# An attention and GLU block on one core: the attention output normalized in its feature layout, the softmax sums spread by DMA, and the GLU weights loaded in 15 parts

## The chip, the core and the metric

The kernel runs on one core of a Trainium2 chip. The core has five engines that each work through a list of instructions in order: TensorE (PE; its weight loads are listed as PEld), VectorE (DVE), ScalarE (ACT), GpSimd (POOL) and SyncE (SP), which in this kernel only issues DMAs. They wait for each other by semaphores. PSUM, the memory that TensorE writes, has eight banks of 128 x 512 fp32. The metric is the device time of one execution in microseconds; the profile shows one execution, and its span is the time from its first to its last instruction.

## What is computed

One sequence of 2048 tokens, 640 features, 32 heads of 20 features, GLU width 1728, all in bf16:

```python
def _A_ref(x, wqkv, wo):                 # 32 heads, Dh = 20
    q, k, v = (x @ wqkv) split by head
    scores = einsum("bhqd,bhkd->bhqk", q, k) * (Dh ** -0.5)
    p = softmax(scores, axis=-1)
    o = einsum("bhqk,bhkd->bhqd", p, v)
    return o.reshape(B, S, D) @ wo
def _B_ref(x, w_gate, w_up, w_down):
    h = gelu(x @ w_gate) * (x @ w_up)
    return h @ w_down
h  = x + _A_ref(layernorm(x), A_wqkv, A_wo)
h2 = h + _B_ref(layernorm(h), B_w_gate, B_w_up, B_w_down)
```

## The kernel before

The kernel is written as a list of operations with their readers and writers, assumed durations and priorities. A planner in Python (`Sched.schedule`) plays them through when the program is built and fixes the order of every engine's list; `Sched.emit` then writes the lists with the semaphore waits that the data need. No time is fixed on the chip: what the planner assumes decides only in which order things stand. An assumed time that is longer makes the planner put more other work ahead of the instruction that waits. For a DMA there are two such times: `dur`, the time of the issue on SP, and `lat`, the time from the issue to the landing. Where PE would be little used, the planner adds filler matmuls ("warm", which stand in the profile as matmuls of `kt_all` with itself, and "pad").

The queries are cut into seven chunks of 512, 512, 256, 256, 256, 128 and 128 tokens. A chunk is worked through in slots: eight groups of four heads for a chunk of 512, two groups together for 256, four for 128, in all 32 slots. In a slot a score tile is 128 keys by 512 query columns; four heads sit in four row quarters of PE (L911). Tiles are taken in units of three and two tiles, 693 units in the kernel. ACT computes the exponential of a unit (a line of a helper, L357, `pts` or `rege` from `ps` with 1536 or 1024 columns). Some tiles are exponentiated by DVE instead (L832 and the TENSOR_SCALAR lines of L357). PE then multiplies by V (L357, 21 columns: 20 features and a column of ones, so that row 20 of each quarter holds the sum of the exponentials). The result for four heads, `O`, collects in PSUM bank 6 as 4 x 32 rows by 512 columns.

When a slot is complete, `epilogue` runs: DVE copies bank 6 to `osb` (fp32, two buffers), PE transposes it in four fp32 transposes (L976), DVE takes the reciprocal of the sums (L982) and multiplies (L985) into `o_nat`, tokens in the partitions.

When all slots of a chunk are complete, `post` runs for it as background of the next chunk: `o_nat` is transposed back to `oT` (features in the partitions), by PE for chunk 0 and for the last, by a transposing DMA otherwise; then the `wo` matmuls (L632) and the residual (L1021), LayerNorm, a transposing DMA of the result to `hnT`, the gate matmuls (L1053, copied out by DVE at L1088), one group of gelus on ACT, the up matmuls (L1053, multiplied at L1099), the down matmuls (L1110), the second residual (L1114) and the store. ACT has to load another table for gelu and again for the exponential. For the last chunk (the tail) the transposes are PE's and the gelu reads PSUM (L1075).

The projections of K, Q and V for groups beyond the first are background of chunk 0: their rows go through DRAM (`k_rows`, `q_rows`) and come back in the layout of the score matmuls, and a bound per query (`bounds`, L724) is added as one more row. All these DMAs are issued by SP in order. In slot 7 the GLU weights are loaded over the place of the QKV weights by three large DMAs and a small one for the last 64 rows of `w_down`, which shares its key and semaphore with the third.

Of the kernel before, what the change touches and what calls it, by code (L numbers as in the profile page):

```python
# [301 lines left out]
D = 640  # L302
# [33 lines left out]
def bass_sequential_preLN__mha_block__glu_gated_geglu__prompt_kernel(  # L336
# [12 lines left out]
    with ExitStack() as es:  # L349
# [3 lines left out]
        def sb(name, shape, dt=BF16):  # L353
            return es.enter_context(nc.sbuf_tensor(name, shape, dt))
# [5 lines left out]
        def c_mm(n, passes=1):  # L360
            return 0.004 + passes * n / 2400.0
# [28 lines left out]
        pts = sb("pts", [128, PR * 512])  # L390
        osb = sb("osb", [128, 2, 512], FP32)
        rc = sb("rc", [128, 2, 16], FP32)
        o_nat = sb("o_nat", [128, 4, D])
        sq = sb("sq", [128, 512])
        xn_t = sb("xn_t", [128, 2, D])

# [51 lines left out]

        kdr = nc.dram_tensor("k_rows", [D, S], BF16, kind="Internal").ap()
        qdr = nc.dram_tensor("q_rows", [4, D, 512], BF16, kind="Internal").ap()  # L450
        odr = nc.dram_tensor("bounds", [4, H, 512], BF16, kind="Internal").ap()

        PS = es.enter_context(nc.psum_tensor("ps", [128, 8 * 512], FP32))
# [135 lines left out]
        def dma_transposes(src, rkeys, dst, wkey, after=()):  # L589
            op("sp", I("dma_start_transpose", dst, src), 1.25, P_EPI, reads=rkeys, writes=[wkey], sem=f"xp{wkey[1]}", lat=2.0, after=after)  # L590
# [364 lines left out]
        def base(c):  # L955
            n = CHUNKS[c][1]
            if n == 128:
                return 2 + (c == len(CHUNKS) - 1)
            return 2 * (c % 2) if n < 512 else 0

        def epilogue(s_, bk):
            s = s_ % 2
            c, gs = slots[s_]
            nq = CHUNKS[c][1]
            nt = nq // 128
            op("dve", I("tensor_copy", osb[:, s, :], PS[:, 512 * 6:512 * 7]), c_dve(512), P_QK,
               reads=[("O", s_)], writes=[("osb", s)], rel=[bk])
            b2 = Bank(*BG[c])
            key = ("bk", sc_id())
            aft = set()  # L970
            tb = base(c)
            for g in gs:
                for tt in range(nt):
                    aft.update(sc.rd.get(("on", g, tb + tt), ()))
            for tt in range(4):
                op("pe", lambda eng, tt=tt: eng.transpose(bank(b2)[:, tt * 128:(tt + 1) * 128],  # L976
                                                          osb[:, s, tt * 128:(tt + 1) * 128], identf[:]),
                   c_mm(128, 2.5), P_EPI, mode="full", reads=[("osb", s), "identf"], writes=[key], acq=[b2] if tt == 0 else [],
                   after=tuple(aft) if tt == 0 else ())
            bv = lambda: bank(b2).rearrange("p (t j e) -> p t j e", t=4, j=4)  # L980
            rcv = rc[:, s, :].rearrange("p (t j) -> p t j", t=4)
            op("dve", lambda eng: eng.reciprocal(rcv, bv()[:, :, :, DH]), 0.17, min(P_EPI, sc.ev), reads=[key], writes=[("rc", s)])  # L982
            for gi, g in enumerate(gs):
                dst = o_nat[:, tb:tb + nt, g * 80:(g + 1) * 80].rearrange("p t (j e) -> p t j e", j=4)
                op("dve", lambda eng, gi=gi, dst=dst: eng.tensor_tensor(  # L985
                    dst, bv()[:, gi * nt:(gi + 1) * nt, :, 0:DH],
                    rcv[:, gi * nt:(gi + 1) * nt, :].unsqueeze(3).to_broadcast([128, nt, 4, DH]), ALU.mult),
                   c_dve(80 * nt), min(P_EPI, sc.ev), reads=[key, ("rc", s)], writes=[("on", g, tb + tt) for tt in range(nt)],
                   rel=[b2] if gi == len(gs) - 1 else [])
# [10 lines left out]
        def post(c, banks, tail):  # L1000
# [3 lines left out]
            tb = base(c)  # L1004
            hb = 1792 * tb
            first = tuple(e_ops) + tuple(last_qk[0]) + tuple(d_ops) if c == 0 else ()
            for tt in range(tb, tb + nt):
                t = q0 // 128 + tt - tb
                i = t % 2
                if tail or c == 0:  # L1010
                    transposes(o_nat[:, tt, :], [("on", g, tt) for g in range(NG)], oT[:, :, tt * 128:(tt + 1) * 128],
                               ("hnT", tt), banks, P_EPI, "act" if tail else "dve", after=first)
                else:
                    dma_transposes(o_nat[:, tt, :], [("on", g, tt) for g in range(NG)], oT[:, :, tt * 128:(tt + 1) * 128],
                                   ("hnT", tt), after=first)
                for hf in range(2):
                    bk = Bank(*banks)
                    key = ("bk", sc_id())
                    list(chain(bk, key, 320, [(oT[:, a, tt * 128:(tt + 1) * 128], wo[:, a, hf * 320:(hf + 1) * 320])
                                              for a in range(NA)], [("hnT", tt), "wo"], p, after=(sc.lw[("h", tt, hf)],)))  # L1020
                    op("dve", lambda eng, bk=bk, tt=tt, hf=hf, i=i: eng.tensor_tensor(  # L1021
                        h_sb[:, tt, hf * 320:(hf + 1) * 320], bank(bk, 320), h_sb[:, tt, hf * 320:(hf + 1) * 320], ALU.add),
                       c_dve(320), p, reads=[key, ("h", tt, hf)], writes=[("h", tt, hf)], rel=[bk], after=first)
                ln_stats(h_sb[:, tt, :], t, [("h", tt, 0), ("h", tt, 1)], p)
# [22 lines left out]
            def mms(k, w, wkey, after):  # L1047
                bk, key = Bank(*banks), ("bk", sc_id())
                for fi in range(min(fn_, NF - k * fn_)):
                    f = k * fn_ + fi  # L1050
                    for a in range(NA):
                        st = fi == 0 and a == 0
                        op("pe", lambda eng, a=a, f=f, fi=fi: eng.matmul(  # L1053
                            bank(bk)[:, fi * nq:(fi + 1) * nq], w[:, a, F0[f]:F0[f] + 128], hnT[:, a, 128 * tb:128 * tb + nq],
                            start=(a == 0), stop=(a == NA - 1)),
                           c_mm(nq), p, mode="full", util=nq / 2400.0, reads=hk + [wkey], writes=[key], acq=[bk] if st else [],
                           after=after if st else ())
                return bk, key

# [6 lines left out]
            def hkeys(k):  # L1066
                return [("ha", u) for u in range((hb + 512 * k) // 256, (hb + 512 * k + cols(k)) // 256)]
# [34 lines left out]
            for tt in range(tb, tb + nt):  # L1102
                t = q0 // 128 + tt - tb
                i = t % 2
                for hf in range(2):
                    bk = Bank(*banks)
                    key = ("bk", sc_id())
                    for f in range(NF):
                        o = hb + f * nq + (tt - tb) * 128
                        op("pe", lambda eng, f=f, o=o, hf=hf, bk=bk: eng.matmul(  # L1110
                            bank(bk, 320), ha_f[:, o:o + 128], wd[:, f, hf * 320:(hf + 1) * 320],
                            start=(f == 0), stop=(f == NF - 1)), c_mm(320), p, mode="full", util=0.133, reads=hkeys(f // fn_) + ["wd", "wdz"],
                           writes=[key], acq=[bk] if f == 0 else [], after=hdone[-2:] if f == 0 else ())
                    op("dve", lambda eng, bk=bk, tt=tt, hf=hf, i=i: eng.tensor_tensor(  # L1114
                        ob[:, i, hf * 320:(hf + 1) * 320], bank(bk, 320), h_sb[:, tt, hf * 320:(hf + 1) * 320], ALU.add),
                       c_dve(320), p, reads=[key, ("h", tt, hf)], writes=[("ob", i, hf)], rel=[bk], after=first)
                op("sp", I("dma_start", out_hbm[t * 128:(t + 1) * 128, :], ob[:, i, :]), 0.08, p,
                   reads=[("ob", i, 0), ("ob", i, 1)], sem=f"out{i}", lat=2.5)
# [17 lines left out]
        for s_, (c, gs) in enumerate(slots):  # L1136
            if c == 0:
# [16 lines left out]
                    q_bound(cc, tuple(range(NA)), 0, NG, BG0, P_BG)  # L1154
                if g == 7:
                    wr = tuple(w_readers)
                    load(wg, B_w_gate.rearrange("(a p) f -> p a f", p=128), "wg", 11.0, after=wr)
                    load(wu, B_w_up.rearrange("(a p) f -> p a f", p=128), "wu", 16.0, after=wr)
                    load(wd[:, 0:NF - 1, :], B_w_down[0:(NF - 1) * 128, :].rearrange("(a p) d -> p a d", p=128),
                         "wd", 21.0, after=wr)  # L1160
                    r0 = (NF - 1) * 128 - F0[-1]
                    load(wd[r0:128, NF - 1, :], B_w_down[(NF - 1) * 128:DFF, :], "wd", 2.6, after=wr)
                    op(POOL, I("memset", wd[0:r0, NF - 1, :], 0.0), 0.8, P_BG, writes=["wdz", "pool"], after=wr)
            while ui < len(units) and uslot[ui] <= s_:
                unit(ui)
# [37 lines left out]
```

## Time and profile before

| | |
|---|---|
| time, median of 3 runs (lowest to highest) | 912.77 us (912.53 to 921.97) |
| the profiled execution: time, span | 915.09 us, 913.2 us |
| mean granted TensorE clock | 0.993 |
| busy in the span: PE, PEld, DVE, ACT, POOL | 861.3, 371.0, 651.7, 859.8, 33.2 us |
| instructions | 24238 |
| exponentials on ACT, first start to last end | 36.1 to 873.2 us |
| bytes moved by DMA | 34.43 MB, mean 38 GB/s |
| fp32 transposes of the epilogue | 128, 26.8 us of PE busy time |
| issue to landing: row stores of 128 KB, load of 640 KB (median) | 1.7 to 1.9 us, 5.2 us |

Busy times of PE overlap with each other, since matmuls are pipelined: a PE that is busy for a whole stretch may still have room. The granted clock is the share of full speed that the throttle let TensorE have. A wait is put down to what ended it. Line numbers are those of the kernel before; L357 is the helper through which many operations are recorded, so that these are told apart by their tiles.

### The profile page before, as it was taken

How to read it: one execution, taken by the hardware profiler on the slowest of the kernel's cores; microseconds unless marked ns; L12 is line 12 of the kernel's file. 1: busy time of each engine (PE TensorE's matmuls, PEld its weight loads, DVE VectorE, ACT ScalarE, POOL GpSimd, SP SyncE). 2: the span in 40 equal slices, each digit the busy share in tenths (PEclk: the TensorE clock that was granted, in tenths of full speed). 3: DMA queues.
4: the chain of work that ended last, by engine and by line, in shares of the span. 5: the costliest groups of instructions: out<-in, count | busy, mean ns of one | idle time of the engine just before them, and what ended most of it. 6: DMA issues, size and time to landing. Idle time of an engine off the chain costs nothing.

```text
span 913.2 us, 24238 instructions
## 1 busy us (share of the span) xinstructions
PE 861.3 (94%) x10905; PEld 371.0 (41%) x10905; DVE 651.7 (71%) x1210; ACT 859.8 (94%) x775; POOL 33.2 (4%) x117
## 2 busy tenths in 40 slices
PE   3999999999999999999999998999999999999998
PEld 2532222222232222222344443333444456666677
DVE  7838797888888968877777785665556766654453
ACT  6699999989999989999999999999999999999960
POOL 5000000000001000000000010000001100010100
PEclk9999999999999989999999999999999999999999
DMA  7211020230100380000100101000101001000100
GB/s 259 86 46 32 13 56 6 61 89 22 50 8 12 64 295 1 1 1 1 31 9 17 38 2 31 1 1 2 38 23 45 17 2 24 25 17 10 39 9 23
DMA packets 39519, 34.43 MB, mean 38 GB/s; under 512 B 19436, under 2 KB 36936, under 8 KB 39416
## 3 DMA queue, kind: packets, MB, share of 16 engines
q1 hardware_dynamic: 39416, 32.89, 12.8%
q8 instruction: 85, 1.39, 0.6%
q14 instruction: 18, 0.15, 0.1%
HBM read 20.12 MB, written 8.09 MB: 31 GB/s over the span
## 4 chain that ended last, share of the span: by engine, by line
PE 46%; ACT 45%; DVE 5%; DMA 2%; issue 0%; SPq 0%; DVEq 0%
ACT pts L357 34%; PE ps L911 13%; PE ps L357 11%; ACT rege L357 10%; PE ps L1053 7%; PE ps L632 7%; PE ps L1110 6%; DMA regw<-in_A_wqkv_dram 1%; DVE rege L832 1%; DVE rege L357 1%; DMA rege<-in_A_x_dram 1%; DVE qt_all L832 1%; ACT L357 1%; PE ps L976 1%; DVE qt_all L357 1%; PE ps L577 0%
## 5 line engine op out<-in xcount | busy, mean ns | idle before, releaser
L357 ACT ACTIVATE pts<-ps 128x1536 bf16<-128x1536 f32 x578 | 652.0, 1252 | 14.8 <-PE ps L911 8.8
L911 PE MATMUL ps<-qt_all,kt_all 32*128 32x256 bf16 (+2 forms) x3584 | 322.4, 290 | 20.2 <-ACT pts L357 11.2
L911 PEld LDWEIGHTS ps<-qt_all,kt_all 32*128 32x128 bf16 x3584 | 102.9, 92 | 236.9 <-ACT pts L357 130.2
L832 DVE TENSOR_SCALAR rege<-ps 128x512 int16<-128x512 f32 x200 | 137.4, 688 | 73.3 <-PE ps L911 71.2
L357 ACT ACTIVATE rege<-ps 128x1536 bf16<-128x1536 f32 x115 | 173.2, 1506 | 1.6 <-PE ps L911 1.1
L1053 PE MATMUL ps<-rege,regw 128*128 128x256 bf16 (+2 forms) x980 | 154.5, 290 | 3.8 <-DVE rege L1099 2.3
L357 PE MATMUL ps<-pts,v_all 128*21 128x256 bf16 (+2 forms) x2472 | 135.0, 288 | 0.0
L357 PE MATMUL ps<-rege,v_all 128*21 128x512 bf16 (+2 forms) x1564 | 127.9, 316 | 1.4 <-DVE rege L357 1.0
L832 DVE TENSOR_SCALAR qt_all<-ps 128x512 int16<-128x512 f32 x116 | 79.8, 688 | 49.1 <-PE ps L911 48.4
L1053 PEld LDWEIGHTS ps<-rege,regw 128*128 128x128 bf16 x980 | 74.3, 98 | 57.8 <-issue 26.1
L357 DVE TENSOR_SCALAR rege<-rege 128x2048 int16<-128x2048 int16 x132 | 88.8, 685 | 2.4 <-PE ps L357 1.1
L632 PE MATMUL ps<-regw 128*128 128x512 bf16 (+1 forms) x360 | 87.5, 352 | 2.0 <-DVE rege L832 0.9
L1110 PE MATMUL ps<-regw,rege 128*128 128x320 bf16 x448 | 80.1, 301 | 1.1 <-DVE rege L832 0.5
L357 PEld LDWEIGHTS ps<-pts,v_all 128*21 128x21 bf16 x2472 | 54.3, 91 | 34.6 <-issue 28.3
L357 PEld LDWEIGHTS ps<-rege,v_all 128*21 128x21 bf16 x1564 | 41.3, 91 | 44.0 <-issue 24.4
L357 PE MATMUL ps<-qt_all,v_all 128*21 128x256 bf16 (+2 forms) x1048 | 53.7, 284 | 2.1 <-DVE qt_all L357 2.0
L1099 DVE TENSOR_TENSOR rege<-rege,ps 128x512 bf16<-128x512 bf16 (+1 forms) x53 | 36.0, 680 | 27.2 <-PE ps L1053 27.2
L1110 PEld LDWEIGHTS ps<-regw,rege 128*128 128x128 bf16 x448 | 37.1, 98 | 29.9 <-issue 13.8
L632 PEld LDWEIGHTS ps<-regw 128*128 128x128 bf16 x360 | 29.2, 99 | 47.6 <-issue 26.3
L1088 DVE CAST rege<-ps 128x512 bf16<-128x512 f32 (+1 forms) x53 | 36.1, 680 | 16.2 <-PE ps L1053 16.0
L357 DVE TENSOR_SCALAR qt_all<-rege 128x2048 int16<-128x2048 int16 x70 | 47.0, 686 | 0.7
L357 DVE TENSOR_SCALAR qt_all<-qt_all 128x2048 int16<-128x2048 int16 x69 | 46.3, 685 | 1.7 <-PE ps L357 1.3
(92 smaller groups left out, 483.7 us busy)
## 6 DMA issues: line engine op xcount, KB each, us to landing
rege<-in_A_x_dram SPq DMA_DIRECT2D x6, 640.0 KB, 5.2
q_rows<-regw SPq DMA_DIRECT2D x20, 128.0 KB, 1.7
out_dram<-rege SPq DMA_DIRECT2D x16, 160.0 KB, 1.9
regw<-in_B_w_gate_dram SPq DMA_DIRECT2D x1, 2160.0 KB, 10.6
regw<-in_B_w_up_dram SPq DMA_DIRECT2D x1, 2160.0 KB, 15.6
regw<-in_B_w_down_dram SPq DMA_DIRECT2D x1, 2080.0 KB, 21.6
kt_all<-k_rows SPq DMA_DIRECT2D x12, 160.0 KB
qt_all<-q_rows SPq DMA_DIRECT2D x12, 160.0 KB
```

The source lines that it names most:

```text
L357: return lambda eng: getattr(eng, method)(*args, **kwargs)
L632: yield op("pe", lambda eng, l=l, r=r, k=k: eng.matmul(bank(bk, n), l, r, start=(k == 0), stop=(k == len(steps) - 1)), c_mm(n), prio, mode ...
L832: d_ops.append(op("dve", lambda eng: eng.tensor_scalar(v[:, 512 * h:512 * h + 512], bank(b), EXP_MUL, -32000.0, ALU.mult, ALU.max), c_dve( ...
L911: return lambda eng: eng.matmul(out()[:, kk * nq:(kk + 1) * nq], kt_all[32 * j:32 * j + 32, g, kt * 128:(kt + 1) * 128], qt_all[32 * j:32 ...
L976: op("pe", lambda eng, tt=tt: eng.transpose(bank(b2)[:, tt * 128:(tt + 1) * 128], osb[:, s, tt * 128:(tt + 1) * 128], identf[:]), c_mm(128 ...
L1053: op("pe", lambda eng, a=a, f=f, fi=fi: eng.matmul(bank(bk)[:, fi * nq:(fi + 1) * nq], w[:, a, F0[f]:F0[f] + 128], hnT[:, a, 128 * tb:128 ...
L1088: cp.append(op("dve", lambda eng, bg=bg, fv=fv, w=w: eng.tensor_copy(fv, bank(bg, w)), c_dve(w), p, reads=[kg], writes=hkeys(k), rel=[bg], ...
L1099: hdone.append(op("dve", lambda eng, bu=bu, fv=fv, w=w: eng.tensor_tensor(fv, fv, bank(bu, w), ALU.mult), c_dve(w), p, reads=[ku] + hkeys( ...
L1110: op("pe", lambda eng, f=f, o=o, hf=hf, bk=bk: eng.matmul(bank(bk, 320), ha_f[:, o:o + 128], wd[:, f, hf * 320:(hf + 1) * 320], start=(f = ...
```

## The change

For all chunks but the last, the epilogue no longer transposes. A new function `spread` works on `osb`, in which the features lie in the partitions: a DMA writes the four rows of sums to DRAM (`sums`), a second loads them back as 128 x 16 (`rc`), DVE takes the reciprocal, a third DMA writes it to DRAM (`rsums`), four DMAs load each row 32 times, once per partition of its quarter (`bsum`), DVE multiplies `osb` by `bsum` into `on16`, and four DMAs write the 20 feature rows of each quarter to DRAM (`attn0` and so on, one per chunk). `post` then loads `oT` from there with one plain DMA in place of the transposes. The planner is told 3.2 us from issue to landing for each of these DMAs, where other loads and stores have 2.2 to 2.7.

The GLU weights are loaded in 15 parts of 128 rows by 1728 (gate and up) or of three blocks of 128 rows by 640 (down). Two parts are under way at a time: part i waits for part i-2. The small last load has a key of its own.

```diff
+        bsum = sb("bsum", [128, 512], FP32)
+        on16 = sb("on16", [128, 512])
-        o_nat = sb("o_nat", [128, 4, D])
+        o_nat = sb("o_nat", [128, 1, D])
...
+        def spread(s, c, gs, nq):
+            n = len(gs)
+            h = lambda dst, src, reads, key, sem, issue: dma(dst, src, key, reads, sem + str(s), 3.2, P_EPI, issue, keep=False)
+            h(sdr[s], osb[DH:128:32, s, :], [("osb", s)], ("sdr", s), "sa", 0.1)
+            h(rc[:, s, :], sdr[s].rearrange("j (a b) -> (j a) b", b=16), [("sdr", s)], ("rc", s), "sb", 0.4)
+            op("dve", I("reciprocal", rc[:, s, :], rc[:, s, :]), 0.25, P_EPI, reads=[("rc", s)], writes=[("rc", s)])
+            h(rdr[s].rearrange("j (a b) -> (j a) b", b=16), rc[:, s, :], [("rc", s)], ("rdr", s), "sc", 0.4)
+            for j in range(4):
+                h(bsum[32 * j:32 * j + 32, :], rdr[s, j].partition_broadcast(32), [("rdr", s)], ("bs", j), "sd", 0.36)
+            op("dve", I("tensor_tensor", on16[:], osb[:, s, :], bsum[:], ALU.mult), c_dve(512), P_EPI,
+               reads=[("osb", s)] + [("bs", j) for j in range(4)], writes=["on16"])
+            for j in range(4):
+                h(adr[c][gs[0]:gs[0] + n, j].rearrange("g e s -> e g s"),
+                  on16[32 * j:32 * j + DH, :].rearrange("p (g s) -> p g s", g=n), ["on16"], ("adr", c, gs[0], j), "se", 0.36)
...
+            if c < len(CHUNKS) - 1:
+                spread(s, c, gs, nq)
+                return
...
+            if not tail:
+                op("sp", I("dma_start", oT[:, :, 128 * tb:128 * tb + nq],
+                           adr[c].rearrange("g j e s -> (g j e) s").rearrange("(a p) s -> p a s", p=128)), 0.4, P_EPI,
+                   reads=[("adr", c, gs[0], j) for cc, gs in slots if cc == c for j in range(4)],
+                   writes=[("hnT", tt) for tt in range(tb, tb + nt)], sem=f"oT{c}", lat=2.4 + nq * 0.001, after=first)
...
-                if tail or c == 0:
-                    transposes(o_nat[:, tt, :], [("on", g, tt) for g in range(NG)], oT[:, :, tt * 128:(tt + 1) * 128],
-                               ("hnT", tt), banks, P_EPI, "act" if tail else "dve", after=first)
-                else:
-                    dma_transposes(o_nat[:, tt, :], [("on", g, tt) for g in range(NG)], oT[:, :, tt * 128:(tt + 1) * 128],
-                                   ("hnT", tt), after=first)
+                if tail:
+                    transposes(o_nat[:, 0, :], [("on", g, 0) for g in range(NG)], oT[:, :, tt * 128:(tt + 1) * 128],
+                               ("hnT", tt), banks, P_EPI, "act", after=first)
...
-                    load(wg, B_w_gate.rearrange("(a p) f -> p a f", p=128), "wg", 11.0, after=wr)
-                    load(wu, B_w_up.rearrange("(a p) f -> p a f", p=128), "wu", 16.0, after=wr)
-                    load(wd[:, 0:NF - 1, :], B_w_down[0:(NF - 1) * 128, :].rearrange("(a p) d -> p a d", p=128),
-                         "wd", 21.0, after=wr)
+                    parts = [(wg[:, a, :], B_w_gate[128 * a:128 * a + 128, :], "wg") for a in range(NA)]
+                    parts += [(wu[:, a, :], B_w_up[128 * a:128 * a + 128, :], "wu") for a in range(NA)]
+                    parts += [(wd[:, f:min(f + 3, NF - 1), :], B_w_down[128 * f:128 * min(f + 3, NF - 1), :].rearrange(
+                        "(a p) d -> p a d", p=128), "wd") for f in range(0, NF - 1, 3)]
+                    ids = []
+                    for i, (dst, src, key) in enumerate(parts):
+                        ids.append(op("sp", I("dma_start", dst, src), 0.35, P_EPI, sem="wp%d" % (i % 2), lat=3.4,
+                                      writes=[(key, i % 2)], after=tuple(wr) if i < 2 else ids[-2:-1]))
...
-                    load(wd[r0:128, NF - 1, :], B_w_down[(NF - 1) * 128:DFF, :], "wd", 2.6, after=wr)
+                    load(wd[r0:128, NF - 1, :], B_w_down[(NF - 1) * 128:DFF, :], "wd2", 2.6, after=wr)
```

The matmuls that read the weights wait for both keys of their weight. Since the planner goes through all operations anew, the order of other work changes too, on every engine.

## The prediction

> **What bounds the kernel now.** I read the page's totals first, then the waits of ScalarE, then stretches of 20 us, then the chain of waits from the end.
>
> ```profile
> PE 861.3 (94%) x10905; PEld 371.0 (41%) x10905; DVE 651.7 (71%) x1210; ACT 859.8 (94%) x775; POOL 33.2 (4%) x117
> ...
> 240.00:260.00 20.00, 18.41 (x171) 5.77 (x171) 16.55 (x30) 20.00 (x18) 0.00 (x0) 1.00 0.16 41
> 320.00:340.00 20.00, 18.93 (x148) 4.30 (x144) 12.33 (x20) 17.37 (x16) 0.00 (x0) 0.81 0.95 329
> 840.00:860.00 20.00, 19.99 (x473) 12.71 (x472) 10.78 (x23) 20.00 (x19) 3.02 (x14) 1.00 0.12 36
> 880.00:900.00 20.00, 19.74 (x219) 15.94 (x217) 9.16 (x22) 6.75 (x8) 0.00 (x0) 1.00 0.05 18
> ```
>
> The columns are stretch, length, PE, PEld, DVE, ACT, POOL, granted clock, DMA share, GB/s. ACT works 20.00 of 20 us in most stretches up to 860: its exponentials are the pace, and PE's projections and GLU matmuls fill gaps behind them. From 873.2 on, when the last exponential ends, ACT falls idle and PE is the bound for the last 40 us. So a cheaper epilogue on PE earns nothing in the middle by itself. It earns where ACT stands still, and in the tail. ACT's stops between the sixth and the last exponential add up to 11 us or so; the large ones are these rows of the timeline (start, length, then idle before and releaser):
>
> ```profile
> 78.98 1.45 ACT L357 ACTIVATE rege<-ps 128x1536 bf16<-128x1536 f32 x1 [1.08 <-PE ps L911]
> 119.24 2.37 ACT L357 ACTIVATE pts<-ps 128x1536 bf16<-128x1536 f32 x2 [1.32 <-PE ps L357]
> 192.12 1.02 ACT L357 ACTIVATE pts<-ps 128x1024 bf16<-128x1024 f32 x1 [3.40 <-PE ps L911]
> 321.65 2.53 ACT L357 ACTIVATE pts<-ps 128x1536 bf16<-128x1536 f32 x2 [1.35 <-PE ps L911]
> ```
>
> The first and the last fall where PE ran at half clock; these windows show it:
>
> ```profile
> 75.00:78.40 3.40, 3.40 (x20) 0.79 (x20) 3.25 (x7) 2.89 (x3) 0.00 (x0) 0.50 0.09 24
> 317.30:320.70 3.40, 3.40 (x20) 0.60 (x17) 2.69 (x5) 3.00 (x3) 0.00 (x0) 0.51 1.05 187
> ```
>
> Four such windows (75, 317, 321 and 328 us) cost ACT 1.08+1.35+0.41+0.75 = 3.6 us, 0.9 each. The stops at 117.9 and 188.7 are of another kind: the order of PE's instructions puts bunches of work between two score matmuls there (next part). The end of the chain of waits (start, length, what):
>
> ```profile
> 871.63 3.12 PE ps L1053 x27
> ...
> 882.46 6.01 PE ps L1110 x44
> 888.47 0.28 PE ps L577 x5
> 888.75 1.63 PE ps L1110 x12
> 890.38 4.63 PE ps L1053 x83
> 895.01 3.81 PE ps L1110 x28
> 898.81 7.11 PE ps L1053 x127
> ```
>
> After the last exponential PE still does the up and down projections of chunk 4 (256-column L1053, and x44+x12 of L1110), then chunk 5's, then chunk 6's.
>
> **The change part by part.** I number an exponential by its place among the 693; they follow each other every 1.13 us (six from 841.20 to 848.00).
>
> *PE.* Removed are 30x4 fp32 transposes (L976; the chain gives 0.44 us for four) and 20 bf16 ones of chunk 0 (0.28 for five): 30x0.44 + 4x0.28 = 14.3 us. Added are 44 filler matmuls (71 instead of 27, about 0.22 us each), which stand where nothing else is ready. While ACT is full this is worth nothing directly: QK goes first anyway. It shows as order. Background ends earlier relative to the exponentials: chunk 3's gelu stands behind exponential 592 instead of 648, chunk 4's behind 667 instead of 692.
>
> *The stop at 117.9.* Before, unit 70's scores are followed by 12 PV matmuls and six projections, 2.6 us by the durations above, against 1.13. In the new order nothing over 1.75 us is found there: -1.3.
>
> *The stop at 188.7.* Before, 18 projection matmuls of 0.22 and 20 PV ones stand between scores 129 and 130, about 4.5 us: slot 6's keys and queries come only then. In the new order the key and query projections of that step stand 4 to 6 places earlier and the bunch is gone: -3.4. The cover is thin: the bounds load behind it in SP's queue now stands past a wait on the first hops and four broadcast issues (4x0.35 us). From DVE's cast at place 122 I count 0.3 + 1.5 (bounds landed in 1.5) + 0.3 + 0.4 + 0.6 + 2 = 5.1 us, ready at place 127 of the 129 needed. If that cover goes, up to 3.4 returns. One new bunch (place 278, 12 PV and 7 GLU matmuls, about 2.5 us) can cost up to 1.3; I take +0.8.
>
> *Tail.* All of ACT's work before the last exponential stays (same exponentials, same gelus, same table loads), so the last exponential at T ends where the stops allow. PE behind T, by count: before 112 of L1110 x 0.136 + 220 x 0.056 + 47 x 0.115 + 3 = 36 us; after about 70 x 0.136 + 260 x 0.056 + 7 fillers + 3 = 28.6. That is 7.4 less. But the chain of the last chunk (PV, copy, transposes, wo, LN, one gelu of chunk 5, two table loads of 1.28) does not shrink with it. Followed instruction by instruction with the rows of before: PV waits for 17 down matmuls and ends at T+1.2 (before T+1.8), wo starts at T+5.6 (T+6.4), chunk 5's gelu ends at T+10.9 (T+11.5), the last LN's transposes at T+13.7 (T+15.1). Behind them stand 24.9 us before. After, 12 fewer L1110 and 48 fewer small L1053: 24.9 - 1.6 - 2.7 = 20.6. End at T+34.1 against 913.2 - 873.2 = 40.0: -5.9. Bounds -3 and -7.4.
>
> *DVE.* Per slot 0.25 + 0.48 to 0.94 us (L982, L985) are replaced by a reciprocal from SBUF (rows 0.17 and 0.25) and a 128x512 product (nearest row 0.685). Over 30 slots that is 26.6 against 24.8 plus the four evictions of 0.48 in chunk 0: nothing.
>
> *SP and the hops.* 330 issues of about 0.35 us are added in 30 slots (11 each: sums out, spread in, reciprocals out, four broadcasts, four outputs), and 6 loads of the normalized output replace 11 transposing DMAs of 1.2 to 1.3 us of issue: about +100 us of a queue that mostly waits. Behind SP's new waits stand key and query writes and the row loads; behind DVE's two new waits (reciprocal, product) its exponentials and evictions stand, and for those PE and ACT wait. DVE's reciprocal stands 7 to 9 places (7.9 to 10.2 us) behind the copy, the product as many behind that. Two hops cost 2 x (0.35 + 1.8) = 4.3 us by the writes of before (landed in 1.7 to 1.9). No row shows a load of 64 B per partition. From above, a store caught behind a 640 KB load at 511 us landed late:
>
> ```profile
> DMA to landing us min/median/max: 4.7/4.7/4.7
> ```
>
> With 4.7, two hops take 10.1, up to 2.2 late, of which one exponential (1.13) is absorbed. I take 1.8 as in most rows, and the late value only for slots 8 and 9, whose hops share the queue with the weights. Four waits there: 0 to +4, taken +0.6.
>
> *Weights.* Three loads issued from 317.5 landed within 10.6, 15.6 and 21.6 us. The first gate matmul stands 29 places after the last gate part's issue, so even a rate halved stays hidden; only hops and clock feel it.
>
> *Clock.* The first cooled window came in a thin stretch (places 29 to 38) that now gets value projections from place 34; the others in thin places 236 to 250 with 7 fillers. Now the thin stretch is 215 to 233 with 13. Bounds: no cooled window, -3.6; eight more, +7; I take -1.3.
>
> Sum: -1.3 - 3.4 + 0.8 - 5.9 + 0.6 - 1.3 = **-10.5 us**. The profiled execution took 915.09 (span 913.2, 1.9 around it): 904.6. It lies 2.3 above the median of 912.77, so I predict **902.3**.
>
> **Rivals.** (1) *Clock windows vanish.* Both spells began right behind fp32 transposes. Without them all 3.6 us would go: 902.3 - 2.3 = **900.0**. Against it: 30 other groups of the same four transposes cooled nothing.
> [...]
>
> (2) *The thin stretch cools.* Places 196 to 234 hold only wo and fillers; eight of its windows at 0.9 us are +7.2 instead of -0.8: **910.3**. For it: 7 fillers did not hold 317 to 331. Against: 16 fillers in places 402 to 440 did, at clock 1.00.
>
> (3) *The stops only move.* Slot 6 is late behind SP's new queue and chunk 0 keeps its stops; only the tail counts: 915.09 - 5.9 - 2.3 = **906.9**.
>
> (4) *Slower: DVE stands at the hops.* If a hop with 64 B rows needs 4.7 us in every slot, the reciprocal is 1.1 to 2.2 and the product 2.2 us late; less 1.13 each, some 1.6 us in each of 30 slots: +48, **950**. It decides from a hop of about 4.1 us on, since two must fit 9 us. For it: no row has such small pieces. Against: every write of 4 to 128 KB landed in 1.5 to 1.9 when alone.
>
> **How the numbers follow.** Forecast 0.50 (898 to 907), rivals 0.13, 0.12, 0.13 and 0.12. Faster by over 1% means under 903.6; 1% is about what a measurement of this kernel can tell from no change. Of the forecast 0.72 lies below (0.36), all of rival 1 and a fifth of rival 3: 0.52. Slower by over 1% is rival 4 alone, 0.12; the rest, 0.36, is within. The range 896 to 914 leaves out rival 4 and a little below.
>
> **What would show it.** Right: no stop of ACT over 1 us near exponentials 69 and 130; last exponential to end 33 to 35 us; chunk 4's up projection (256 columns) all before the last exponential; hops landing in 1.5 to 2.5 us and no DVE wait on DMA beyond slots 8 and 9. Wrong: DVE idle before the reciprocal or the product in most slots, more than four half-clock windows, or a tail of 38 us and more.

## The result, and the profile after

The changed kernel took 928.29 us (median of 4 runs, 923.64 to 932.81) against 912.70 us for the kernel before on the same chip: a ratio of 1.0155 with a 95% interval of 1.0115 to 1.0195. It is slower by 1.6%, where I had forecast 902.3 us. (In all ratios here, runs more than 1.5% above their kernel's fastest are left out.) The profiled execution is the fastest of the four, 923.64 us, 8.55 above the profiled one of before.

The page's first lines and its clock row (40 slices of 23 us, granted TensorE clock in tenths, 9 is 90% or more):

```profile
span 921.9 us, 24386 instructions
...
PE 862.8 (94%) x10813; PEld 358.9 (39%) x10813; DVE 648.7 (70%) x1188; ACT 862.3 (94%) x775; POOL 32.8 (4%) x117
...
PEclk9996999999999799999989999999999999999999
```

The busy sums say nothing: each engine is within 3 us of before (PEld aside, which shrinks by 12). The clock row does: three dents. The mean granted clock is 0.974, before 0.993. Three of the stretches shown for the kernel before (columns: stretch, length, PE, PEld, DVE, ACT, POOL, clock, DMA share, GB/s):

```profile
240.00:260.00 20.00, 19.14 (x167) 5.28 (x159) 17.09 (x31) 19.95 (x19) 0.00 (x0) 1.00 0.26 71
320.00:340.00 20.00, 19.34 (x160) 5.16 (x157) 16.72 (x28) 20.00 (x18) 0.00 (x0) 0.99 0.06 17
840.00:860.00 20.00, 17.91 (x393) 11.72 (x391) 10.17 (x18) 19.94 (x18) 2.10 (x12) 1.00 0.09 18
```

Where the clock is full, ACT is as busy as before. ScalarE's timeline at the two stops that the new order was to remove (start, length, form; an idle time would stand in brackets):

```profile
119.64 4.75 ACT L357 ACTIVATE pts<-ps 128x1024 bf16<-128x1024 f32 x4
...
189.05 5.54 ACT L357 ACTIVATE pts<-ps 128x1024 bf16<-128x1024 f32 x5
```

They are gone. The same view in the first dent:

```profile
78.93 1.45 ACT L357 ACTIVATE rege<-ps 128x1536 bf16<-128x1536 f32 x1 [1.52 <-PE ps L916]
...
83.20 3.86 ACT L357 ACTIVATE pts<-ps 128x1536 bf16<-128x1536 f32 x3 [1.78 <-PE ps L916]
87.69 1.02 ACT L357 ACTIVATE pts<-ps 128x1024 bf16<-128x1024 f32 x1 [0.64 <-PE ps L916]
89.95 1.45 ACT L357 ACTIVATE rege<-ps 128x1536 bf16<-128x1536 f32 x1 [1.23 <-PE ps L916]
```

One stop behind another, all released by scores (L916). The windows around this dent and the next:

```profile
71.10:74.50 3.40, 2.39 (x20) 0.67 (x20) 3.35 (x9) 3.40 (x4) 0.00 (x0) 1.00 0.47 135
74.50:77.90 3.40, 3.40 (x21) 0.72 (x18) 3.06 (x7) 2.91 (x3) 0.00 (x0) 0.50 0.01 5
...
303.20:306.60 3.40, 1.41 (x11) 0.39 (x11) 3.13 (x8) 1.90 (x3) 0.00 (x0) 1.00 0.28 54
306.60:310.00 3.40, 2.92 (x29) 0.66 (x26) 2.25 (x4) 2.12 (x3) 0.00 (x0) 0.50 0.58 125
```

A window with little work on PE (2.39 and 1.41 us) is followed by half clock. The trace has 14 such cold windows of 3.41 us: five from 74.5, one at 129.1, four from 306.6, three from 477.3, one at 825.4. Before there were four. ACT's stops over 0.3 us in and right behind them add up to 15.9 us, before 3.6. (The stop of 1.50 us at 305.94 ends before its cold spell begins and is not in this sum.) The last exponential ends at 887.07 instead of 873.24.

The second dent has a cause of its own. VectorE's waits for DMA (us in total, times, longest), and the instruction in its timeline:

```profile
DVE rc L357 <- DMA rc<-sums: 3.4, 2, 2.9
DVE on L357 <- DMA bsum<-rsums: 1.3, 1, 1.3
```

```profile
303.39 0.25 DVE L357 RECIPROCAL rc<-rc 128x16 f32<-128x16 f32 x1 [2.88 <-DMA rc<-sums]
```

```profile
305.94 1.45 ACT L357 ACTIVATE rege<-ps 128x1536 bf16<-128x1536 f32 x1 [1.50 <-PE ps L916]
```

While weight parts were under way, one hop was late; DVE stood 2.88 us at the reciprocal, a DVE exponential behind it (L837, at 304.44) was late, PE stood 2.54 us for that, ACT 1.50 us for PE, and the cold spell from 306.6 followed. That is the only long wait for a hop. The other hops are short (count, size, median us from issue to landing):

```profile
bsum<-rsums SPq DMA_DIRECT2D x120, 64.0 KB, 2.1
...
rc<-sums SPq DMA_DIRECT2D x30, 8.0 KB, 2.3
rsums<-rc SPq DMA_DIRECT2D x30, 8.0 KB, 1.4
```

The end of the chain of waits (start, length, what):

```profile
898.59 2.85 PE ps L1078 x48
...
903.68 3.81 PE ps L1135 x28
907.49 7.11 PE ps L1078 x127
```

The up projection of chunk 4 is no longer behind the last exponential; from there to the end it is 34.84 us (921.91 - 887.07), before 39.95.

### The profile page after: what moved, and what is told of

It is laid out like the page before. It is cut to its first block, busy times and chain, and to the rows that moved or that the text cites. A ratio compares the mean times of both kernels' runs of the same rounds, so it can differ in the third digit from the quotient of the medians.

```text
span 921.9 us, 24386 instructions
## 1 busy us (share of the span) xinstructions
PE 862.8 (94%) x10813; PEld 358.9 (39%) x10813; DVE 648.7 (70%) x1188; ACT 862.3 (94%) x775; POOL 32.8 (4%) x117
## 4 chain that ended last, share of the span: by engine, by line
ACT 52%; PE 40%; DMA 4%; DVE 3%; issue 1%; SPq 0%; DVEq 0%
ACT pts L357 39%; PE ps L916 12%; ACT rege L357 12%; PE ps L357 10%; PE ps L1078 8%; PE ps L1135 5%; PE ps L637 4%; DMA regw<-in_B_w_up_dram 1%; DMA regw<-in_B_w_gate_dram 1%; ACT L357 1%; DMA regw<-in_B_w_down_dram 1%; DVE stats L357 1%; DVE rege L837 1%; PE ps L582 1%; DMA rege<-attn 0%
## 5 line engine op out<-in xcount | busy, mean ns | idle before, releaser
L916 PE MATMUL ps<-qt_all,kt_all 32*128 32x256 bf16 (+2 forms) x3584 | 324.3, 293 | 22.8 <-ACT pts L357 14.9
L916 PEld LDWEIGHTS ps<-qt_all,kt_all 32*128 32x128 bf16 x3584 | 102.2, 92 | 245.8 <-ACT pts L357 139.2
L837 DVE TENSOR_SCALAR rege<-ps 128x512 int16<-128x512 f32 x200 | 137.2, 688 | 78.1 <-PE ps L916 76.2
L1078 PE MATMUL ps<-rege,regw 128*128 128x256 bf16 (+2 forms) x980 | 157.4, 290 | 6.4 <-ACT rege L357 3.6
L357 PE MATMUL ps<-pts,v_all 128*21 128x256 bf16 (+2 forms) x2472 | 137.6, 293 | 0.1
L357 PE MATMUL ps<-rege,v_all 128*21 128x512 bf16 (+2 forms) x1564 | 132.4, 321 | 1.4 <-DVE rege L357 1.3
L837 DVE TENSOR_SCALAR qt_all<-ps 128x512 int16<-128x512 f32 x116 | 79.8, 688 | 45.6 <-PE ps L916 44.6
L637 PE MATMUL ps<-regw 128*128 128x512 bf16 (+1 forms) x360 | 90.2, 359 | 1.6 <-ACT regw L588 0.4
L1135 PE MATMUL ps<-regw,rege 128*128 128x320 bf16 x448 | 82.9, 302 | 1.4 <-DVE rege L1124 0.6
L357 PEld LDWEIGHTS ps<-pts,v_all 128*21 128x21 bf16 x2472 | 54.7, 92 | 34.1 <-issue 26.2
```

The lines of the kernel that those rows point to most:

```text
L357: return lambda eng: getattr(eng, method)(*args, **kwargs)
L637: yield op("pe", lambda eng, l=l, r=r, k=k: eng.matmul(bank(bk, n), l, r, start=(k == 0), stop=(k == len(steps) - 1)), c_mm(n), prio, mode ...
L837: d_ops.append(op("dve", lambda eng: eng.tensor_scalar(v[:, 512 * h:512 * h + 512], bank(b), EXP_MUL, -32000.0, ALU.mult, ALU.max), c_dve( ...
L916: return lambda eng: eng.matmul(out()[:, kk * nq:(kk + 1) * nq], kt_all[32 * j:32 * j + 32, g, kt * 128:(kt + 1) * 128], qt_all[32 * j:32 ...
L1078: op("pe", lambda eng, a=a, f=f, fi=fi: eng.matmul(bank(bk)[:, fi * nq:(fi + 1) * nq], w[:, a, F0[f]:F0[f] + 128], hnT[:, a, 128 * tb:128 ...
L1135: op("pe", lambda eng, f=f, o=o, hf=hf, bk=bk: eng.matmul(bank(bk, 320), ha_f[:, o:o + 128], wd[:, f, hf * 320:(hf + 1) * 320], start=(f = ...
```

## The experiments

My theory after the traces (A): the removed fp32 transposes were work that kept TensorE's clock up in the thin places of the middle, and without them the clock falls. Rivals: (B) the hops or the part loads cost the time; (C) transposes do not count for the clock, and something else in the new order cools it. A *thin place* is counted from the order of the instructions: three units in a row (3 x 1.13 us by the pace of the exponentials, about one cold window) whose columns on PE come to less than 1.2 us. The 1.2 us are an estimate of mine, and the counts at the end of this document bear it out only roughly: they put the edge at 0.32 to 0.42 of 3.41 us, which is 1.1 to 1.4. A matmul of 512 columns counts 0.213 us, the planner's `util` for it (the trace of before has 0.216 from one start to the next), and a quarter of that where four share the array (there four start 3 to 4 ns apart, and the next four 0.22 us later). An fp32 transpose of 128 columns counts as much as 512 columns, an estimate (the 26.8 us of PE busy time over 128 of them are 0.209 each). Counted by this rule in the order of the programs, the kernel before has 5 such places and the changed one 12. (The expectations below put the changed kernel at 18, and at 9 and 4 with other allowances; the same count gives 5 and 2 for those two.) Left out of the count altogether, the transposes leave the kernel before with 46 thin places.

The rule prices a transpose too high, and so do the expectations that give transposes and matmuls the same column time. The chain of the kernel before shows what four in a row take:

```profile
842.50 0.44 PE ps L976 x4
```

One behind another, the fp32 transposes start 0.109 us apart; bf16 ones (in the bf16 run of the kernel before, below) start 0.055 apart, and bf16 matmuls of 512 columns 0.216. Four fp32 transposes thus take 0.44 us and not 0.85. At 0.109 each, the kernel before still has 5 thin places.

### The transposes put back as dead work, and each half of the change alone

```diff
 e1:             spread(s, c, gs, nq)
+                b2, key = Bank(*BG[c]), ("bk", sc_id())
+                for tt in range(4):
+                    op("pe", lambda eng, tt=tt: eng.transpose(bank(b2)[...], osb[:, s, ...], identf[:]), c_mm(128, 2.5), P_EPI, ...)
 e2: the same with
+                    op("pe", lambda eng: eng.matmul(bank(b2), kt_all[:, 0, 0:128], kt_all[:, 0, 0:512], ...), c_mm(512), P_EPI, ...)
 e3 (from the changed kernel), and e4 the other way round (from the kernel before):
-                    parts = [...]          # 15 loads
+                    load(wg, ...); load(wu, ...); load(wd[:, 0:NF - 1, :], ...)
```

> The changed kernel with the four fp32 transposes of each attention slot put back on TensorE, their result read by nobody (they add work; nothing is left out). Theory A (the removed transposes were the TensorE work that kept its clock up): the cold windows fall from 14 (47.8 us) to 6 or fewer, the granted clock rises from 0.974 to 0.985 or more, and the time is 905 to 913 us. Rival B (the 15 part loads, or the longer hops, cost the time): it stays at 920 us or more. Rival C (transposes do not count for the clock): clock at or below 0.978, 920 us or more.

Measured: 922.81 us (920.46 to 928.01), ratio 1.0110 (1.0072 to 1.0148), clock 0.987 in the profiled run, 7 cold windows. The clock rose as theory A says, but the time did not fall to 913: it lies where rivals B and C put it. In this new order the planner put the transposes elsewhere, and the windows ahead of all three spells (127.0, 492.2 and 789.2) held none of them. This run alone decides nothing.

> The changed kernel with four bf16 matmuls of 512 columns in each attention slot, in the place of the transposes (the same column time, 0.85 us a slot; they add work, nothing is left out). Theory A: as with the fp32 transposes, 905 to 913 us, at most 6 cold windows. Rival C (only true matmuls keep the clock up): this one mends the clock and the kernel with transposes does not, 8 us or more between the two. Rival B: 920 us or more, like the changed kernel.

Measured: 913.21 us (909.56 to 918.17), ratio 0.9998 (0.9978 to 1.0018); no cold window in the profile, clock 1.000. So 15 us of the loss went with the clock, and rival B falls as the main cause: hops and part loads are all there. The 120 added matmuls were not free: the tail is 37.39 us. Rival C's sign came true as well: this run is 9.6 us below the one with transposes. But an added matmul takes twice the time of a transpose (0.216 us against 0.109), and each of the two kernels got an order of its own from the planner, so the pair does not decide; the tests in an unchanged order further down do.

> The normalization in the feature layout alone: the weights by three loads and one, as before. TensorE's thin places by order are those of the changed kernel (18). Theory A: 920 to 932 us, a clock of 0.960 to 0.978, 10 or more cold windows. Rival B1 (the 15 part loads cost the time): 903 to 912 us.

Measured: 935.93 us, ratio 1.0253 (1.0207 to 1.0299), clock 0.963. Slower than the changed kernel, so the parts are no loss but a cure. ACT's, DVE's and SP's timelines show of what:

```profile
308.04 1.02 ACT L357 ACTIVATE pts<-ps 128x1024 bf16<-128x1024 f32 x1 [9.52 <-PE ps L916]
```

```profile
304.64 0.69 DVE L357 TENSOR_TENSOR on<-osb,bsum 128x512 bf16<-128x512 f32 x1 [9.68 <-DMA bsum<-rsums]
```

```profile
285.51 8.48 SPq L357 DMA_DIRECT2D rsums<-rc  x1
301.27 1.73 SPq L357 DMA_DIRECT2D bsum<-rsums  x4
```

Behind three large loads, issued at 280 to 282, the store of the reciprocals took 8.48 us to issue, and the broadcasts, which need it landed, went out at 301.27. DVE stood 9.68 us, ACT 9.52.

> The kernel before with the weights in 15 parts, two under way; transposes and DVE's normalization as before. Theory A: within 4 us of the kernel before, 909 to 916 us, 6 cold windows or fewer. Rival B1 (the part loads cost the time): 920 us or more.

Measured: 914.86 us, ratio 1.0013 (0.9997 to 1.0030). Without hops the part loads are worth nothing either way.

### The kernel before with less heat, and with more

*Heat* is here a name for work on PE that keeps the clock up; no run measures a temperature.

```diff
 e6 (from the kernel before):
-        osb = sb("osb", [128, 2, 512], FP32)
+        osb = sb("osb", [128, 2, 512])
-                op("pe", ... eng.transpose(bank(b2)[...], osb[...], identf[:]), ...)
+                op("pe", ... eng.transpose(bank16(b2, 512)[...], osb[...], ident[:]), ...)
 e7 (from the kernel before): at the end of epilogue
+            if c < 3: two matmuls of 512 columns into a bank of BG[c]
```

> The kernel before, in its own order of instructions, with one thing changed: the four transposes of each slot are taken in bf16 instead of fp32, 0.21 us of columns instead of 0.85 (the denominators and outputs are rounded to bf16 one step earlier). No hops, no loads in parts. Theory A: the heat that kept the clock up is gone; 8 cold windows or more, clock 0.980 or lower, 917 to 930 us. Rival C (transposes do not count): as the kernel before, 910 to 915 us, at most 5 cold windows.

Measured: 921.00 us (914.57 at a clock of 0.990 to 930.94 at 0.965), ratio 1.0060 (1.0035 to 1.0086); in the profile 11 cold windows, clock 0.980. This is the cleanest of the tests: every engine's order is that of before, the transposes are still there, only each takes half the time on PE (0.055 us instead of 0.109). Two windows that had stayed warm before with four fp32 transposes in them (first the whole window, then the transposes alone):

```profile
341.20:344.60 3.40, 3.12 (x22) 0.98 (x21) 1.83 (x5) 3.40 (x4) 0.00 (x0) 1.00 0.09 24
389.00:392.40 3.40, 3.26 (x28) 1.03 (x25) 2.71 (x7) 3.40 (x4) 0.00 (x0) 1.00 0.00 0
```

```profile
341.20:344.60 3.40, 1.10 (x4) 0.48 (x4) 1.00 0.09 24
389.00:392.40 3.40, 0.88 (x4) 0.45 (x4) 1.00 0.00 0
```

and the first of them in this run, with the window behind it:

```profile
341.90:345.30 3.40, 2.63 (x25) 0.70 (x17) 2.02 (x5) 3.40 (x4) 0.00 (x0) 1.00 0.00 0
345.40:348.80 3.40, 3.40 (x21) 0.73 (x18) 2.19 (x4) 2.64 (x3) 0.00 (x0) 0.50 0.00 0
```

PE's busy time falls from 3.12 to 2.63 us, and the clock halves. Rival C, for which this edit changes nothing, falls.

> The kernel before with two bf16 matmuls of 512 columns added per slot of chunks 0 to 2: the kernel before at a clock that stays up, so that the change can be priced at an even clock. Theory A: at most 2 cold windows, 908 to 913 us, and 2 to 6 us above the changed kernel with heat in chunks 0 to 2. If the change gains nothing at an even clock, the two are within 1 us.

Measured: 929.18 us, ratio 1.0171 (1.0147 to 1.0196). A miss, and no control: the planner's new order had two stops of 7.1 and 7.2 us (the second where PE waited 6.6 us for a transposing DMA that stood behind the weights), and 10 cold windows, two of them in the second stop.

### Heat only in the early chunks; the allowance for the hops

> The changed kernel with four bf16 matmuls of 512 columns per attention slot as in the run before, but only for chunks 0 to 2 (they add work, nothing is left out), so that TensorE's work behind the last score product is as in the changed kernel. Theory A: no more than 3 cold windows, the last exponential ends near 871 us as with the heat in all slots, and the tail is 34 to 36 us: 905 to 910 us. If the 37.4 us tail of the run with heat in all slots came from something other than the added matmuls: 910 to 915 us. If the change has a cost beside the clock that the stops and the tail do not pay back: 912 us or more.

The edit is that of the bf16 run above under `if c < 3:`. Measured: 910.94 us (909.40 to 915.85), ratio 0.9977 (0.9960 to 0.9993), two cold windows, tail 34.84 us. The tail is back at the changed kernel's, so the longer one came from the added matmuls. The time missed the expected 910 by 0.9: PE waited 1.7 us for a transposing DMA from 313.6 on, and the two cold windows began within that wait, at 314.2.

```diff
 e8:
-            h = lambda ...: dma(dst, src, key, reads, sem + str(s), 3.2, P_EPI, issue, keep=False)
+            h = lambda ...: dma(dst, src, key, reads, sem + str(s), 2.0, P_EPI, issue, keep=False)
 e13: 2.6 in the same place, and two matmuls per slot under "if c < 3:"
```

> The changed kernel with 2.0 us allowed for each hop instead of 3.2. Thin places by order 9 instead of 18. Theory A: some of the cold spells go, 5 to 11 cold windows, 910 to 924 us. If the allowance matters for the waits (hops that land later than planned hold DVE or TensorE): DVE waits for DMA grow from 4.7 us to 20 us or more and the time is 925 us or more.

Measured: 927.98 us, ratio 1.0137 (1.0102 to 1.0171), 16 cold windows. The time is where the second theory put it: DVE's waits for the hops grew from 4.7 to 19.1 us (14 times, longest 2.8). Theory A missed: the clock, 0.971 in the profile, is no better.

> The changed kernel with 2.6 us allowed for each hop instead of 3.2 and two bf16 matmuls per slot of chunks 0 to 2. By order 4 thin places. Theory A: as with four matmuls and 3.2 us, 906 to 912 us, at most 4 cold windows. If a shorter allowance brings waits at the hops (as the kernel with 2.0 us showed 2.9 us in one place): 914 us or more with the clock mended.

Measured: 929.37 us, ratio 1.0163 (1.0123 to 1.0203), clock 0.976, DVE's waits for the hops 4.8 us. Miss: few thin places (4 by the expectation, 2 by the rule above), but 13 cold windows, in spells at 73.6, 121.4 and 285.2. How much of it is the allowance and how much the order that it gives isn't settled by these two runs; neither is better than 3.2.

### Heat without a change of order

```diff
 e9 (from the changed kernel, 88 units), e11 (from the kernel before, 58 units): ahead of the score matmuls
+            if u in HEAT:
+                fns.append(lambda eng: eng.matmul(PS[:, 512 * s0:512 * s0 + 512], kt_all[:, 0, 0:128], kt_all[:, 0, 0:512], ...))
 e10: the same units
+                fns.append(lambda eng: eng.transpose(PS[:, 512 * s0:512 * s0 + 128], identf[:], identf[:]))
```

> The changed kernel in its own order of instructions on every engine; ahead of the score products of 88 of the 693 units, those around the places where TensorE's columns are thin, one more bf16 matmul of 512 columns is put into the bank that the scores then overwrite (0.213 us of columns each; nothing is left out). Theory A: the clock is what the change lost, so 2 to 5 cold windows, clock 0.99 or more, 905 to 911 us. Rival B (hops or loads hold the kernel up beside the clock): 915 us or more, with the clock mended.

Measured: 922.26 us (916.85 to 932.49), ratio 1.0110 (1.0072 to 1.0148). The clock in the profile is 1.000 with no cold window but at its very last 0.4 us, as theory A has it, but the time is 11 us above what it gave, where rival B put it.

> The kernel before in its own order, with the same added matmul at 58 units around its own thin places: the kernel before at a clock that stays up, to price the change at an even clock. Theory A: at most 2 cold windows, 909 to 913 us, and 2 to 6 us above the changed kernel with heat. If the change is worth nothing at an even clock: within 1 us of it.

Measured: 922.78 us, ratio 1.0086 (1.0064 to 1.0108), clock 0.994. Both theories missed, by 10 us, and the miss shows where those 11 us can have gone: ahead of the scores a matmul is not free. 58 of them cost the kernel before, which has no hops, 9.2 us at its usual clock, 0.16 each. If they cost the changed kernel as much, 88 make 14, and 922.3 - 14 = 908 for the change with the clock mended. Neither run prices the change directly.

> As the run before, but the added instruction is one fp32 transpose of 128 columns at the same 88 units (the same column time, 0.213 us). Theory A (fp32 transposes keep the clock up as matmuls do): within 3 us of the run with matmuls. Rival C (transposes do not count): 10 or more cold windows, clock below 0.98, 920 us or more.

Measured: 924.18 us (918.41 to 929.26), 1.9 above the run with matmuls; clock 0.994 in the profile, three cold windows. The profiled execution is the fastest of six, though: over all six the median clock is 0.985 with transposes, 0.995 with matmuls and 0.969 in the changed kernel's four. So fp32 transposes do hold the clock up, the second blow to rival C, but in the same 88 places less than matmuls of twice their time (0.216 us against 0.109). That the times come out so near may be because a shorter instruction also costs less ahead of the scores; no run separates the two.

### Little heat, and heat in the right places

> The changed kernel with one bf16 matmul of 512 columns per slot of chunks 0 to 2 instead of four (20 in all, 4.3 us of columns; nothing is left out). By order 4 thin places. Theory A (the clock is the loss, and a little heat in the thin slots mends it): 4 cold windows or fewer, 906 to 911 us, at or below the kernel with four. If the four matmuls a slot were needed for the clock (a dose effect): 8 or more cold windows, 914 to 924 us.

The edit is that of the early-chunk run with one matmul per slot. Measured: 913.31 us, from 906.50 at a clock of 0.996 to 919.62 at 0.980; ratio 0.9996 (0.9972 to 1.0020). The median missed the expected 911. The profiled execution had 10 cold windows: eight behind its thin places 29, 37, 235 and 411, and two at 271 behind a 2.4 us stop of PE at the first `wo` matmul, whose 640 KB load took 6.1 us while weight parts were moving. With that many windows this run does not exclude the dose effect. Its 12 runs lie about a line: 904.5 us at full clock (within 2.6), and 7.5 us more for each 0.01 of clock lost. Three of the changed kernel's four runs lie near the same line (0.974: 924.0 by the line, 923.64 measured; 0.963: 932.3 and 931.91; 0.960: 934.5 and 932.81), the fourth is 3.6 us above it (0.978: 921.0 and 924.68). The 84 runs of the kernel before that stand beside these experiments give 911.2 us at full clock (within 0.4) and 5.0 us per 0.01.

```diff
 e14 (from e12):
+            if u in (28, 29, 30, 36, 37, 38, 234, 235, 236, 410, 411, 412): a matmul of 512 columns ahead of the scores, as in e9
-                   ... sem=f"oT{c}", lat=2.4 + nq * 0.001, after=first)
+                   ... sem=f"oT{c}", lat=(5.5 if c == 0 else 2.4) + nq * 0.001, after=first)
```

> The changed kernel with one bf16 matmul per slot of chunks 0 to 2 as in the run with a quarter of the heat, 12 more such matmuls ahead of the score products of the units around its four thin places (29, 37, 235, 411), three of which went cold there, and 5.5 us instead of 2.4 allowed for the first chunk's attention load, for which TensorE stood 2.4 us while weight parts were under way. Nothing is left out. Theory A: at most 2 cold windows, clock 0.993 or more, 905 to 909 us, below both kernels. If the cold is not made by thin places: as the run with a quarter of the heat, 911 to 916 us, clock near 0.989.

Measured: 905.64 us (904.36 to 915.32), ratio 0.9920 (0.9896 to 0.9945): faster than both kernels. Windows of its profile around the place of the first dent:

```profile
69.00:72.40 3.40, 3.40 (x26) 0.89 (x23) 3.31 (x7) 3.24 (x4) 0.00 (x0) 1.00 0.11 39
72.40:75.80 3.40, 3.01 (x24) 0.75 (x21) 2.80 (x8) 3.40 (x4) 0.00 (x0) 1.00 0.48 130
```

```profile
PEclk9999999999999999999999999999999999999999
```

32 matmuls, 6.8 us of columns in all, hold the clock at 1.00 through the whole profiled execution, as 120 spread over the slots did: the place counts, not the dose alone. ACT's stops fall from 21.9 us to 5.3. The two edits went in together, so their shares aren't told apart.

## Why the prediction was wrong

By its own steps:

- *Stop at 117.9* (-1.3) and *stop at 188.7* (-3.4): right, both are gone. The cover at place 127 held.
- *Bunch at place 278* (+0.8): right in kind; ACT stands 1.20 us there.
- *Tail* (-5.9): right; -5.1 (34.84 us, forecast 34.1), chunk 4's up projection ahead of the last exponential as said. (13.7 + 20.6 is 34.3, so the term should have read -5.7.)
- *Hops* (+0.6, in slots 8 and 9 alone): right as a wait, 4.7 us of DVE in three waits, the long one beside the weights, and 1.50 us of ACT right behind that. What was missed is the price: that wait let TensorE cool, and the spell behind it holds 4.3 us more of ACT's stops.
- *Weights* (hidden): right for the matmuls. For the hops the parts are needed: without them one hop costs 9.5 us.
- *Clock* (-1.3, bounds -3.6 and +7): wrong, and this is the step that failed: -1.3 was taken between the bounds without a working. Measured from the stops it is 15.9 - 3.6 = +12.3 in the profiled execution, the fastest of the four, and beyond the upper bound.

Without the clock's term my sum was -9.2. Read at full clock, the change with 20 added matmuls is 904.5 - 911.2 = -6.7; the placed run, 6 of whose 9 executions are at 1.000, is 905.3 - 911.2 = -5.9 with 32. The rest of the sum thus held to some 3 us, as far as kernels with added matmuls show it. In the changed kernel the gaps cost a little more than their length: ACT's time between the sixth and the last exponential without its gaps grew from 817.2 to 819.8 us. Consecutive exponentials overlap by about 0.15 us, and an added gap, of which there are 25, can lose that.

The wrong sentence stands a part earlier: the removed transposes are "worth nothing directly" while ACT is full. I costed them as time on PE and not as heat. Four fp32 transposes of a slot take 0.44 us, an eighth of a window, and without them the kernel before would have 46 thin places instead of 5. Rival 2 (the thin stretch cools) had the mechanism, but for places 196 to 234 alone, where the added fillers are; the cold came at 31 to 42, 77, 227 to 235, 365 to 371 and 647. Four of these five spells lie at or behind thin places (28 to 38, 68 to 72, 359 to 362, 637 to 639) that counting columns in the new order shows beforehand; the one at rival 2's stretch follows the late hop. Not every thin place went cold (131 and 194 did not), so the count names candidates. (Rival 2's price also takes the clock term as -0.8, where the sum has -1.3.) I had counted PE's instructions by number and not by columns.

Rival 1 had the sign wrong. I gave it 0.13 on two spells which began behind transposes. This case's traces speak against it for fp32: over 14 traces, among windows at full clock in which the other columns fill under 0.36 of the window, 53 of 59 with two or more fp32 transposes in them were followed by full clock, and 19 of 54 with at most one. In five of these traces about a tenth of the records of wide matmuls is missing; in the other nine it is 35 of 39 and 11 of 38. A window is here one of 3.41 us, as the cold spells show it: in the changed kernel's trace those of 17.07 and 13.65 us are five and four of it, and in the traces of both kernels the spells begin on one grid of such windows (in the changed kernel 16, 68, 118 and 220 of them after the first at 74.48, each within 0.001 of a window).

Rival 4 (DVE stands at every hop) was excluded by median landings of 1.4 to 2.3 us; only an allowance of 2.0 us brought some of it, 19.1 us of waits.

## What to carry to other kernels

Before taking work off an engine that is "not the bottleneck", ask what else that work did: here it held TensorE's clock (0.993 in the profile of before, 0.980 with the same transposes in bf16). Count columns per 3.41 us, the length of a cold window in these traces, in the new order, with the spacing that the trace shows for each kind of instruction; where they fill under 0.36 of it (of such windows here with at most one fp32 transpose, 35 of 54 were followed by a cold one), put a few dead matmuls there. Where the planner has room they cost less than ahead of the work on the path: with 120 in the slots of the changed kernel the executions at a clock of 1.000 took 909.6 to 910.2 us, with 88 ahead of the scores 916.9. Where small hops share a queue with bulk loads, try the bulk in parts: here it spared a wait of 9.5 us.

## What the runs showed of the hardware

- fp32 transposes of 128 columns against an identity follow one another 0.109 us apart in the kernel before, bf16 ones 0.055 us apart, bf16 matmuls of 512 columns 0.216.
- fp32 transposes hold the granted clock up: in the same 88 places they bring the median clock from 0.969 to 0.985, bf16 matmuls of twice the time to 0.995, and taking the transposes of the kernel before in bf16 gave 11 cold windows instead of 4 and 0.6% more time.
- The edge lies between 0.32 and 0.42 of a window of 3.41 us in these traces, and it is not sharp: of the windows at full clock with at most one fp32 transpose, 22 of 28 whose other columns filled under 0.32 were followed by a cold one, 13 of 26 from 0.32 to 0.36, 6 of 70 from 0.36 to 0.42, and none of 3037 above.
- One cold window costs this kernel about 1.1 us of ACT's stops (15.9 us over 14), less than the 1.7 us of PE that half of its 3.41 us makes. PE's slack behind ACT may take up the rest; no run shows that. By the lines of time against clock it is 0.9 us in the kernel before and 1.4 us in the run with 20 added matmuls.
- A store of 8 KB issued behind three loads of about 2 MB each took 8.5 us to issue; in the changed kernel the same store takes 0.34 us (median of 30).
